# A planner that knows PSUM banks, whole-bank rows, one Strassen product later, and new places for parts of y

## The chip, the cores and the metric

The kernel runs on one core of a Trainium2 chip. The metric is the device time of one execution in microseconds. The median of three runs of the kernel before is 859.1 us (858.09 to 859.74).

## What is computed

The reference is block-causal attention followed by two feed-forward parts, in float32, on 2304 tokens of 512 features:

```python
# q, k, v: 4 batches, 8 heads, 576 positions, 64 features; blocks of 64 positions
attn = softmax(where(pos_i // 64 >= pos_j // 64, q @ k.T / 8, -1e9)) @ v
x = attn reshaped to (2304, 512)
h = (x @ w1) * (x @ w2) @ w3          # 512 -> 1024 -> 1024
x = h @ w_out                         # -> 512, called y in the kernel
h = x @ w_in                          # -> 2048
out = (relu(h) ** 2) @ w_out2         # -> 512
```

w3 and w_out are multiplied with each other first, so that the middle part is one product of the gate with that 1024 by 512 matrix.

## The kernel before, in words

**Precision.** A float32 operand is split into a high part (a copy on ScalarE) and a low part (a subtraction on VectorE), and a product is three matmuls: high by high, high by low, low by high. Every tensor that a matmul reads has therefore been through ScalarE and VectorE.

**Stages.** First the weights come in and are converted, and the eight rows of w3 times w_out (`setup_rows`, L1173) are computed, in between the attention of the first batch. Each row is a product of 128 by 512 elements that is accumulated in PSUM and then evicted: a copy on ScalarE (L1209) and a subtraction on VectorE (L1214). Rows 0 to 5 use one PSUM bank, `po`, one after the other; rows 1 to 5 are computed as two halves of 256 columns of that bank, rows 0, 6 and 7 whole. The first three rows have plain float32 operands, the others split ones. Then the first feed-forward part runs for each batch (`ab_products`, `y_products`) beside the attention of the next; y goes to DRAM.

The second feed-forward part (`second_block`, L1369 on) takes y in five blocks: block 0 of 256 tokens, blocks 1 to 4 of 512. For each pair of hidden rows j (0 to 7) a block makes a group of products. Block 0 makes them directly, blocks 1 to 4 by Strassen's scheme with seven products (`h_winograd`, L1842): P1, P7, P2, P6, P4, P5, P3 in the order of the code, each of six matmuls of 256 columns. They go into four PSUM banks in halves: `b17` has P1 on the left and P7 on the right, `b26` has P2 and P6, `b45` has P4 and P5, `b3` has P3. In blocks 2 to 4 the banks come from a ring of three (`bank3`), so P3 of a group takes the bank of P1 and P7, and P1 of the next group that of P2 and P6. ScalarE copies P1 out to `x1` (L1904), VectorE makes two sums `c1` of x1 with P6 and with P2, then `u3` out of P7 and c1, and so on (all at L1898). Blocks 2 to 4 also use Strassen's scheme for the second product (`out_strassen`, the o products, L2034).

The seven operands that a block needs of y (`b11`, `b21`, `t1`, `t2`, `t4`, `b22`, `t3`, each as high and low part) are made by `y_load` (L1522): four subtractions (L1543) and seven splits (`y_split`, L1413, by the helper at L275 and L277). Each has one buffer for all blocks, so block c+1 writes b11 only when block c has read it for the last time. The raw y of a block lies in two of four buffers (`raw`), which the output of a block uses too.

**What sets the order.** All work is written as operations with an engine, a cost, a key and lists of what they read and write (`Order.op`, L97 on). `Order.emit` (L117) plans them once, in Python, before the program exists: it goes through time with those costs and, whenever an engine is free, gives it the ready operation with the smallest key. The order in which it does so is the order of the instructions on each engine. An operation is ready when those that it depends on are done; dependencies are kept per key, and a key can be a part of a tile, such as one half of a bank. Evictions have the key `K_EVICT`, ahead of everything; in blocks 2 to 4 the adds have `K_EVICT - 1`. The work of step n of the second part has keys from K_B + 2n.

```python
start = max(t0, min(o.ready for o in todo))
o = min((o for o in todo if o.ready <= start), key=lambda o: (o.key, o.n))
```

The semaphores of the program are set afterwards from the order of the instructions, by PSUM bank and not by half.

Of the kernel before, what the change touches and what calls it, by code (L numbers as in the profile page):

```python
# [44 lines left out]
    return 128 * t + 64  # L45


class Buf:


# [16 lines left out]
class Op:  # L67
    def __init__(self, eng, cost, fn, key, spare):
        self.eng, self.cost, self.fn, self.key, self.spare = eng, cost, fn, key, spare
        self.deps = set()  # L70
        self.left = 0
        self.users = []
        self.ready = 0.0
        self.end = None


class Order:
# [19 lines left out]
    def op(self, eng, cost, fn, r=(), w=(), key=0.0, spare=0.0):  # L97

        o = Op(eng, cost, fn, key, spare)
        o.same = self.same.get(eng, 0.0)  # L100
        for k in r:
            if k in self.writer:
                o.deps.add(self.writer[k])
            self.readers.setdefault(k, []).append(o)
        for k in w:
            if k in self.writer:
                o.deps.add(self.writer[k])
            o.deps.update(self.readers.pop(k, ()))
            self.writer[k] = o
        for k in list(r) + list(w):  # L110
            if isinstance(k[0], Buf):
                k[0].ops.append(o)
        o.deps.discard(o)
        self.ops.append(o)
        return o

    def emit(self):  # L117
# [7 lines left out]
        for o in self.ops:  # L125
            o.left = len(o.deps)
            for d in o.deps:
                d.users.append(o)
        free, avail, dma = {}, {}, 0.0
        for n, o in enumerate(self.ops):  # L130
            o.n = n
            if not o.left:
                avail.setdefault(o.eng, []).append(o)
        count = 0
        while True:
            best = None
            for eng, todo in avail.items():
                if not todo:
                    continue
                t0 = free.get(eng, 0.0)  # L140
                start = max(t0, min(o.ready for o in todo))
                o = min((o for o in todo if o.ready <= start), key=lambda o: (o.key, o.n))
                if best is None or start < best[0]:
                    best = (start, o, eng)
            if best is None:
                break
            start, o, eng = best
            if eng == "P" and self.idle:
                self.idle(start - free.get(eng, 0.0))
            avail[eng].remove(o)  # L150
            count += 1
            if isinstance(o.cost, tuple):
                issue, move, late = o.cost
                free[eng] = start + issue
                dma = max(dma, start + issue) + move
                o.end = dma + late
            else:
                free[eng] = start + o.cost
                o.end = free[eng] + self.TAIL.get(eng, 0.0)
            o.fn()  # L160
            for u in o.users:
                u.left -= 1
                same = u.eng == eng and eng in "PAV"
                u.ready = max(u.ready, free[eng] + u.same if same else o.end + self.WAIT + u.spare)
                if not u.left:
                    avail.setdefault(u.eng, []).append(u)
# [4 lines left out]
def fused_kernel(ctx: ExitStack, tc: tile.TileContext, qT, kT, vp, va, w12, w3t, wo, wb, out):  # L171
# [1001 lines left out]
    def setup_rows(i):  # L1173
# [3 lines left out]
            w3o_t.append(w8_buf(8 + i // 2, f"w3o_{i // 2}"))  # L1177
        if not i:
            po_bank.append(buf("pm", "po", 1, [P, 512], F32, "po"))
        for half in range(2) if 0 < i < PO_SPLIT else (None,):  # L1180
            cols = slice(0, 512) if half is None else slice(256 * half, 256 * half + 256)
            n = cols.stop - cols.start
            if i < PO_SPLIT:
# [185 lines left out]
    def second_block():  # L1369
# [31 lines left out]
            return late("hx", [P, 512], name, F32, 1, "mb")  # L1401

        ys_ = {}
        raws_ = {}
        r_ = {}
        cp_ = {}

        def y_part(c, name):

            home = "wp" if name in ("b11", "b21") else "w2"  # L1410
            return [late(f"{name}{n}", [P, 2, TH], f"{name}{n}_{c}", F16, 1, home) for n in "hl"]

        def y_split(c, name, src, key):  # L1413
            h, l = ys_[c, name] = y_part(c, name)
            split_half(h, l, src, 2 * TH, ([(h,)], [(l,)], [key]), K_EVICT)

        def y_raw(c, key):

# [103 lines left out]
        def y_load(c):  # L1522
# [17 lines left out]
            def sub(o, x, y, r, w):  # L1540
                od.op(
                    DVE, c_dve(2 * TH),
                    lambda: dve.tensor_tensor(out=o(), in0=x(), in1=y(), op=ALU.subtract), r, w, K_EVICT,  # L1543
                )

            sub(t1, b12, b11, [k12, k11], [(t1,)])
# [19 lines left out]
        def both(f, half):  # L1566
            return [wkey(f, x, half) for x in "hl"]
# [192 lines left out]
        def h_direct(c, j, key):  # L1760
            gt = g_half(c, j, f"g2_{c}_{j}")
            bt = beta_a if j < SOON else beta
            for k in range(2):
# [8 lines left out]
                            start=n == 0, stop=n == len(mms) - 1,  # L1772
                        )

                ks = both(f, 0) + [(t,) for x in ("b11", "b21") for t in ys_[c, x]]
                od.op(PE, len(mms) * c_mm16(TH), go, ks, [(acc,)], key)
                x = buf("mo1", "a", 2, [P, GMAX], F32, f"r_{f}")
                od.op(
# [63 lines left out]
        def h_winograd(c, j, key):  # L1842
# [16 lines left out]
            def product(acc, half, left, yname, spare=0.3):  # L1859
# [8 lines left out]
                            start=n == 0, stop=n == len(mms) - 1,  # L1868
                        )

                od.op(PE, len(mms) * c_mm16(TH), go, ks + [(t,) for t in y], [(acc, half)], key, spare * strassen)

            if strassen:
                c3 = late("c", [P, 3, TH], f"c3_{c}_{j}", F32, 2)
# [24 lines left out]
                )  # L1899

            product(b17, 0, w_of(0, 0), "b11")
            product(b17, 1, s_of(3), "t3")
            od.op(
                ACT, c_act(TH), lambda: act.activation(x1(), half_of(b17, 0)(), AF.Copy), [(b17, 0)], [(x1,)], K_OUT  # L1904
            )
            product(b26, 0, w_of(0, 1), "b21")
            product(b26, 1, s_of(2), "t2")
            if strassen:
                add(TH, half_of(c1, 1), half_of(b26, 1), x1, [(b26, 1), (x1,)], ck[1:])
            else:  # L1910
# [431 lines left out]
```

## Time and profile before

| | us |
|---|---|
| median of three runs | 859.1 |
| lowest and highest | 858.09, 859.74 |
| the profiled execution | 859.63 |
| its span in the profile | 857.9 |
| TensorE matmuls busy | 834.0 (97%) |
| VectorE busy | 704.3 (82%) |
| ScalarE busy | 605.3 (71%) |

The span runs from the first instruction to the end of the last; the execution's own time has 1.7 us around it. In the rows below PE is TensorE's matmuls, PEld its weight loads, DVE is VectorE, ACT ScalarE, POOL GpSimd, which here mostly issues transfers. A row of the timeline has the start and the length in us, the engine, the line of the kernel, the operation, what it writes and reads by name, shape and count, and in brackets how long its engine had been idle and what ended that. Matmul rows last longer than their spacing, since matmuls overlap.

### The profile page before, as it was taken

What the parts mean: (1) busy time and instruction counts of PE and PEld (TensorE: products, weight loads), DVE (VectorE), ACT (ScalarE), POOL (GpSimd) and SP (SyncE); (2) the same over time, 40 slices, a digit from 0 to 9 for tenths busy, and PEclk for the clock granted to TensorE, in tenths of its full rate; (3) what the DMA queues carried; (4) which work ended last, traced back from release to release, by engine and by line L of the source; (5) the groups of instructions that cost most, each with busy time, mean ns of one, the idle gap of its engine ahead of it and who ended that gap; (6) DMA issues with size and microseconds to landing.
All of it is one profiled execution on the core that took longest, in us unless ns stands there. A gap on an engine that the chain in (4) does not pass through costs nothing. (4 is left out here: it accounts for less than half of the span.)

```text
span 857.9 us, 19317 instructions
## 1 busy us (share of the span) xinstructions
PE 834.0 (97%) x7504; PEld 676.9 (79%) x7504; DVE 704.3 (82%) x1643; ACT 605.3 (71%) x1393; POOL 111.4 (13%) x206
## 2 busy tenths in 40 slices
PE   8999999999999999999999999999999999999997
PEld 6567776778878888789979878666678888888886
DVE  5988989997787787864788899999979798797775
ACT  5988888976677676764999985756755654664562
POOL 5111211111211112001322101010020001001000
PEclk9999999999999999999999999999999999999999
DMA  8942465699998999772665512020030002001001
GB/s 312 339 150 93 135 176 161 143 182 191 215 178 159 196 154 202 134 148 77 210 193 191 176 50 74 26 100 2 1 109 16 1 2 74 2 1 51 1 2 50
DMA packets 104830, 100.23 MB, mean 117 GB/s; under 512 B 83041, under 2 KB 86881, under 8 KB 103329
## 3 DMA queue, kind: packets, MB, share of 16 engines
q0 software_dynamic: 18144, 71.18, 26.5%
q1 hardware_dynamic: 86592, 27.80, 19.1%
q8 instruction: 59, 0.97, 0.5%
q14 instruction: 35, 0.28, 0.1%
HBM read 62.78 MB, written 9.44 MB: 84 GB/s over the span
## 5 line engine op out<-in xcount | busy, mean ns | idle before, releaser
L1108 PEld LDWEIGHTS <-w 128*128 128x128 f16 x1536 | 146.8, 98 | 43.7 <-issue 5.9
L884 ACT ACTIVATE pf<-s,nm 128x192 f32<-128x192 f32 (+4 forms) x160 | 82.4, 524 | 44.0 <-DVE nm L867 39.5
L1108 PE MATMUL ab<-x0h,w 128*128 128x320 f16 x512 | 108.9, 299 | 0.5 <-DVE w L287 0.3
L1108 PE MATMUL y<-g,w3o 128*128 128x320 f32 (+1 forms) x768 | 108.3, 298 | 0.0
L1108 PEld LDWEIGHTS y<-g,w3o 128*128 128x128 f32 x768 | 103.1, 188 | 2.1 <-issue 1.2
L1108 PE MATMUL ab<-x1h,w 128*128 128x256 f16 x512 | 88.7, 273 | 0.0
L2034 PEld LDWEIGHTS <-gs 128*128 128x128 f16 x816 | 78.9, 98 | 11.4 <-DVE gs L277 2.2
L1866 PEld LDWEIGHTS <-wb 128*128 128x128 f16 x768 | 75.1, 98 | 15.2 <-issue 3.8
L1108 PE MATMUL ab<-x0l,w 128*128 128x320 f16 x256 | 76.5, 299 | 0.7 <-DVE x0l L1033 0.7
L1929 ACT ACTIVATE c<-c,beta 128x512 f32<-128x512 f32 x48 | 34.2, 713 | 58.4 <-DVE c L1898 58.4
L932 DVE SCALAR_TENSOR_TENSOR p<-pf,r,p 128x192 f16<-128x192 f32 (+2 forms) x120 | 63.0, 546 | 12.5 <-ACT p L925 11.2
L1108 PE MATMUL ab<-x1l,w 128*128 128x256 f16 x256 | 69.8, 272 | 0.0
L2161 PE MATMUL o<-wb,g 128*128 128x512 f16 x288 | 66.7, 379 | 0.6 <-DVE c L2171 0.6
L925 ACT ACTIVATE p<-pf,r 128x192 f16<-128x192 f32 (+2 forms) x120 | 62.0, 556 | 6.6 <-DMA pt<-p 3.7
L2034 PE MATMUL p<-ts,gs 128*128 128x256 f16 x480 | 61.8, 273 | 0.1
L1866 PEld LDWEIGHTS <-st 128*128 128x128 f16 x576 | 56.1, 98 | 6.7
L825 PE MATMUL s<-kraw,qraw 64*128 64x288 f32 (+4 forms) x384 | 56.5, 411 | 0.4 <-ACT pf L884 0.2
L2161 PEld LDWEIGHTS <-g 128*128 128x128 f16 x288 | 27.9, 98 | 30.3 <-issue 0.9
L825 PEld LDWEIGHTS s<-kraw,qraw 64*128 64x128 f32 x384 | 34.2, 186 | 17.1 <-issue 8.3
L2034 PE MATMUL p<-wb,gs 128*128 128x256 f16 x336 | 44.7, 273 | 0.2 <-DVE gs L277 0.2
L859 DVE TENSOR_REDUCE nm<-s 128x2 f32<-128x384 f32 (+1 forms) x64 | 42.3, 683 | 1.0
L338 DVE CUSTOM_DVE_ANT_0 cx<-raw,cx 128x1024 uint16<-128x1024 uint16 (+1 forms) x53 | 39.0, 737 | 4.5 <-ACT raw L329 2.3
(265 smaller groups left out, 1977.4 us busy)
## 6 DMA issues: line engine op xcount, KB each, us to landing
raw<-in_wb POOLq DMA_DIRECT2D x32, 512.0 KB, 5.5
raw<-in_w3t POOLq DMA_DIRECT2D x8, 1024.0 KB, 10.0
raw<-in_w POOLq DMA_DIRECT2D x16, 512.0 KB, 4.8
yraw<-ydram POOLq DMA_DIRECT2D x12, 512.0 KB, 4.5
vraw<-in_vp POOLq DMA_DIRECT2D x16, 320.0 KB, 5.3
qraw<-in_qT POOLq DMA_DIRECT2D x16, 288.0 KB, 4.7
kraw<-in_kT POOLq DMA_DIRECT2D x32, 144.0 KB, 5.9
vmix<-v SPq DMA_DIRECT2D x24, 160.0 KB, 5.0
```

Of the source, the lines that this page charges most:

```text
L338: dve.tensor_tensor(out=x(), in0=x(), in1=words()[1], op=ALU.add)
L825: pe.matmul(o[:, h] if t == 4 else o, q()[rows, q_start(t) : q_start(t) + 128], keys_()[rows, c], start=True, stop=True,)
L859: lambda k=k, t=t, nm=nm, banks=banks: dve.tensor_reduce(out=nm()[:, k], in_=banks[0]()[:, :, S_COL[t] : S_COL[t] + n_keys(t)], op=ALU.max ...
L884: act.activation(o, view(a, t), AF.Exp, bias=nm()[:, k, a : a + 1], scale=SCALE, accum_out=ssum()[:, k, a : a + 1],)
L925: lambda o=o, nk=nk, a=a, k=k, w=weights, p16=p16, r=r: act.activation(p16()[:, o : o + nk], w(a, k), AF.Copy, scale=r()[:, k, a : a + 1]),
L932: lambda o=o, nk=nk, a=a, k=k, w=weights, p16=p16, r=r: dve.scalar_tensor_tensor(out=p16()[:, o + nk : o + 2 * nk], in0=w(a, k), scalar=r( ...
L1108: pe.matmul(acc(), l, r, start=k == 0, stop=k == len(mms) - 1)
L1866: pe.matmul(acc()[:, TH * half : TH * half + TH], lhs(a, kc), y[yn]()[:, kc], start=n == 0, stop=n == len(mms) - 1,)
L1929: lambda src=src, k=k: act.activation(src(), src(), AF.Relu, scale=beta()[:, j, k : k + 1]),
L2034: pe.matmul(acc()[:, TH * u : TH * u + TH], t()[:, o : o + P], r(b), start=first and n == 0 and u == tiles[0], stop=last and n == 2 and u ...
L2161: pe.matmul(o(), g[gx]()[:, cols], wt(f)[:, a, 512:1024], start=(begin and n == 0), stop=(last and n == 2),)
```

## The change

It has four parts. The planner remembers, for each PSUM bank, until when TensorE writes it and until when the other engines use it: an operation of TensorE starts after the others are through with all of its bank, and one of another engine after TensorE's writes to any part of that bank. Rows 1 to 5 of w3 times w_out are computed in whole banks. P7 stands behind P6 in the code of a group. For block 3, b11, b21 and t3 get places of their own, in buffers that nothing else uses by then; and the subtractions and splits of y for blocks 3 and 4 have a key behind step 5 of the block before instead of `K_EVICT`.

```diff
--- before.py
+++ after.py
@@ -45,6 +45,9 @@
     return 128 * t + 64
 
 
+PSUM_POOLS = ("ps", "pm", "mb")
+
+
 class Buf:
 
 
@@ -68,6 +71,7 @@
     def __init__(self, eng, cost, fn, key, spare):
         self.eng, self.cost, self.fn, self.key, self.spare = eng, cost, fn, key, spare
         self.deps = set()
+        self.banks = ()
         self.left = 0
         self.users = []
         self.ready = 0.0
@@ -111,6 +115,7 @@
             if isinstance(k[0], Buf):
                 k[0].ops.append(o)
         o.deps.discard(o)
+        o.banks = tuple(dict.fromkeys(k[0] for k in (*r, *w) if isinstance(k[0], Buf) and k[0].pool in PSUM_POOLS))
         self.ops.append(o)
         return o
 
@@ -127,6 +132,14 @@
             for d in o.deps:
                 d.users.append(o)
         free, avail, dma = {}, {}, 0.0
+        written, read = {}, {}
+
+        def at(o):
+            t = o.ready
+            for b in o.banks:
+                t = max(t, (read if o.eng == "P" else written).get(b, 0.0))
+            return t
+
         for n, o in enumerate(self.ops):
             o.n = n
             if not o.left:
@@ -138,8 +151,8 @@
                 if not todo:
                     continue
                 t0 = free.get(eng, 0.0)
-                start = max(t0, min(o.ready for o in todo))
-                o = min((o for o in todo if o.ready <= start), key=lambda o: (o.key, o.n))
+                start = max(t0, min(at(o) for o in todo))
+                o = min((o for o in todo if at(o) <= start), key=lambda o: (o.key, o.n))
                 if best is None or start < best[0]:
                     best = (start, o, eng)
             if best is None:
@@ -157,6 +170,9 @@
             else:
                 free[eng] = start + o.cost
                 o.end = free[eng] + self.TAIL.get(eng, 0.0)
+            for b in o.banks:
+                d = written if eng == "P" else read
+                d[b] = max(d.get(b, 0.0), o.end + self.WAIT)
             o.fn()
             for u in o.users:
                 u.left -= 1
@@ -1177,7 +1193,7 @@
             w3o_t.append(w8_buf(8 + i // 2, f"w3o_{i // 2}"))
         if not i:
             po_bank.append(buf("pm", "po", 1, [P, 512], F32, "po"))
-        for half in range(2) if 0 < i < PO_SPLIT else (None,):
+        for half in (None,):
             cols = slice(0, 512) if half is None else slice(256 * half, 256 * half + 256)
             n = cols.stop - cols.start
             if i < PO_SPLIT:
@@ -1401,18 +1417,39 @@
             return late("hx", [P, 512], name, F32, 1, "mb")
 
         ys_ = {}
+        K_LOAD = [K_EVICT if c < 3 else K_B + 2 * (KP * (c - 1) + 5) + 0.55 for c in range(len(BLOCKS))]
         raws_ = {}
         r_ = {}
         cp_ = {}
 
+        OTHER_HOMES = {
+            "b11": ("wp", "ysq", 1, 1), "b21": ("wp", "ysc", 1, 1), "t3": ("mo1", "a", 2, 2),
+        }
+
+        class Piece:
+            def __init__(self, b, n):
+                self.b, self.n, self.key = b, n, (b, n)
+
+            def __call__(self):
+                return self.b()[:, self.n]
+
+        def key_of(t):
+            return t.key if isinstance(t, Piece) else (t,)
+
         def y_part(c, name):
 
+            if c == FIRST_S + 1 and name in OTHER_HOMES:
+                *home, pieces = OTHER_HOMES[name]
+                if pieces == 2:
+                    return [buf(*home, [P, 2, TH], F16, f"{name}{n}_{c}") for n in "hl"]
+                t = buf(*home, [P, 2, 2, TH], F16, f"{name}_{c}")
+                return [Piece(t, n) for n in range(2)]
             home = "wp" if name in ("b11", "b21") else "w2"
             return [late(f"{name}{n}", [P, 2, TH], f"{name}{n}_{c}", F16, 1, home) for n in "hl"]
 
         def y_split(c, name, src, key):
             h, l = ys_[c, name] = y_part(c, name)
-            split_half(h, l, src, 2 * TH, ([(h,)], [(l,)], [key]), K_EVICT)
+            split_half(h, l, src, 2 * TH, ([key_of(h)], [key_of(l)], [key]), K_LOAD[c])
 
         def y_raw(c, key):
 
@@ -1540,7 +1577,7 @@
             def sub(o, x, y, r, w):
                 od.op(
                     DVE, c_dve(2 * TH),
-                    lambda: dve.tensor_tensor(out=o(), in0=x(), in1=y(), op=ALU.subtract), r, w, K_EVICT,
+                    lambda: dve.tensor_tensor(out=o(), in0=x(), in1=y(), op=ALU.subtract), r, w, K_LOAD[c],
                 )
 
             sub(t1, b12, b11, [k12, k11], [(t1,)])
@@ -1772,7 +1809,7 @@
                             start=n == 0, stop=n == len(mms) - 1,
                         )
 
-                ks = both(f, 0) + [(t,) for x in ("b11", "b21") for t in ys_[c, x]]
+                ks = both(f, 0) + [key_of(t) for x in ("b11", "b21") for t in ys_[c, x]]
                 od.op(PE, len(mms) * c_mm16(TH), go, ks, [(acc,)], key)
                 x = buf("mo1", "a", 2, [P, GMAX], F32, f"r_{f}")
                 od.op(
@@ -1868,7 +1905,7 @@
                             start=n == 0, stop=n == len(mms) - 1,
                         )
 
-                od.op(PE, len(mms) * c_mm16(TH), go, ks + [(t,) for t in y], [(acc, half)], key, spare * strassen)
+                od.op(PE, len(mms) * c_mm16(TH), go, ks + [key_of(t) for t in y], [(acc, half)], key, spare * strassen)
 
             if strassen:
                 c3 = late("c", [P, 3, TH], f"c3_{c}_{j}", F32, 2)
@@ -1899,12 +1936,12 @@
                 )
 
             product(b17, 0, w_of(0, 0), "b11")
-            product(b17, 1, s_of(3), "t3")
             od.op(
                 ACT, c_act(TH), lambda: act.activation(x1(), half_of(b17, 0)(), AF.Copy), [(b17, 0)], [(x1,)], K_OUT
             )
             product(b26, 0, w_of(0, 1), "b21")
             product(b26, 1, s_of(2), "t2")
+            product(b17, 1, s_of(3), "t3")
             if strassen:
                 add(TH, half_of(c1, 1), half_of(b26, 1), x1, [(b26, 1), (x1,)], ck[1:])
             else:
```

## Rows read from the trace of the kernel before

**Rows 1.** The page's part 1, busy time of each engine.

```profile
PE 834.0 (97%) x7504; PEld 676.9 (79%) x7504; DVE 704.3 (82%) x1643; ACT 605.3 (71%) x1393; POOL 111.4 (13%) x206
```

**Rows 2.** The table of windows: busy us of each engine, TensorE's granted clock, DMA.

```profile
36.00:64.00 28.00, 24.70 (x128) 17.70 (x129) 22.88 (x43) 23.89 (x45) 3.67 (x6) 0.94 0.49 167
64.00:124.00 60.00, 58.15 (x473) 46.45 (x470) 51.47 (x131) 50.03 (x135) 10.50 (x20) 1.00 0.42 126
124.00:200.00 76.00, 71.12 (x684) 55.72 (x683) 70.29 (x191) 62.76 (x158) 11.99 (x23) 1.00 0.76 165
200.00:600.00 400.00, 397.95 (x3763) 320.81 (x3760) 325.63 (x790) 296.00 (x731) 60.96 (x111) 1.00 0.62 141
600.00:840.00 240.00, 237.09 (x2078) 202.17 (x2077) 197.44 (x405) 143.43 (x263) 9.46 (x16) 1.00 0.07 23
690.00:700.00 10.00, 8.75 (x81) 7.68 (x80) 9.96 (x21) 3.80 (x8) 0.00 (x0) 1.00 0.01 2
700.00:765.00 65.00, 65.00 (x594) 57.47 (x593) 52.84 (x111) 39.50 (x73) 2.91 (x5) 1.00 0.08 26
```

**Rows 3.** Waits of TensorE: us in total, times, longest us.

```profile
PE p L1866 <- DVE c L1898: 2.9, 3, 1.3
...
PE po L1108 <- DVE w3o L1214: 2.4, 5, 0.6
...
PE pv_bank L357 <- DVE wsum L406: 1.7, 2, 1.3
```

**Rows 4.** Timeline of an ordinary group of block 2: start us, us, instruction [idle before].

```profile
665.90 0.27 PE L1866 MATMUL p<-b11h,wb 128*128 128x256 f16 x1
...
666.55 0.27 PE L1866 MATMUL p<-t3h,st 128*128 128x256 f16 x1
...
666.86 0.39 ACT L1904 ACTIVATE x<-p 128x256 f32<-128x256 f32 x1 [0.53 <-PE p L1866]
```

**Rows 5.** Timeline of the turn from block 2 to block 3.

```profile
690.63 0.68 DVE L1543 TENSOR_TENSOR yraw<-yraw,t 128x512 f32<-128x512 f32 x1
...
690.67 0.36 ACT L1904 ACTIVATE x<-p 128x256 f32<-128x256 f32 x1
...
691.57 0.41 DVE L1898 TENSOR_TENSOR c<-p,x 128x256 f32<-128x256 f32 x1
...
691.90 0.68 DVE L1940 TENSOR_TENSOR s<-c 128x512 f32<-128x512 f32 x1
...
692.50 0.41 DVE L1898 TENSOR_TENSOR c<-p,x 128x256 f32<-128x256 f32 x1
...
692.96 0.27 PE L1866 MATMUL p<-b11h,wb 128*128 128x256 f16 x1 [1.25 <-DVE c L1898]
...
695.91 0.68 DVE L277 TENSOR_TENSOR t3l<-yraw,t3h 128x512 f16<-128x512 f32 x1
```

**Rows 6.** Timeline of the rows' stage, VectorE, ScalarE and TensorE.

```profile
36.84 0.61 ACT L1209 ACTIVATE w3o<-po 128x512 fp32r<-128x512 f32 x1
...
37.93 0.69 DVE L1214 TENSOR_TENSOR w3o<-po,w3o 128x512 fp32r<-128x512 f32 x1
...
45.20 0.38 ACT L1209 ACTIVATE w3o<-po 128x256 fp32r<-128x256 f32 x1 [0.81 <-PE po L1108]
...
45.63 1.13 PE L1108 MATMUL po<-wox,w3x 128*128 128x256 f32 x4 [0.47 <-ACT w3o L1209]
...
46.87 0.42 DVE L1214 TENSOR_TENSOR w3o<-po,w3o 128x256 fp32r<-128x256 f32 x1 [1.59 <-PE po L1108]
```

**Rows 7.** Timeline of TensorE, two runs of row matmuls.

```profile
73.58 2.35 PE L1108 MATMUL po<-wo,w 128*128 128x256 f32 x18
...
113.97 7.28 PE L1108 MATMUL po<-wo,w 128*128 128x512 f32 x30
```

**Rows 8.** The page's part 5, ScalarE's longest kind in the Strassen blocks.

```profile
L1929 ACT ACTIVATE c<-c,beta 128x512 f32<-128x512 f32 x48 | 34.2, 713 | 58.4 <-DVE c L1898 58.4
```


## The prediction

> **What bounds the kernel now.** I read the page's busy time first: TensorE's matmuls cover 834.0 of 857.9 us of span [rows 1]. So all that can be won without less matmul work is the 23.9 us in which TensorE is idle, and the question is where these lie and which of them the change touches. The table of windows answers the first half [rows 2]: 36 to 64 us has 3.3 us idle (28.0 less 24.7), 64 to 124 has 1.85, 124 to 200 has 4.9, the 400 us after that 2.05, and 600 to 840 has 2.9; what is left (about 9 us) is the start before 36 us and the tail after 840 us, which the change hardly reaches. VectorE is second: nearly full at 124 to 200 (70.3 of 76 us), 82% busy from 600 to 840.
>
> The table of waits names the idle stretches [rows 3]: the Strassen products wait for VectorE's adds at L1898, 2.9 us in 3 times; the rows of w3 times w_out wait for VectorE's eviction at L1214, 2.4 us in 5; the small norm matmul waits for wsum, 1.7 us in 2. The first is all of the idle time of 600 to 840.
>
> Two stretches of the timeline show why. In an ordinary group [rows 4] P1 (b11) writes the left half of bank p17 and its last matmul starts at 665.90; ScalarE's copy of that half starts only at 666.86, when P7 (t3), which writes the right half, has had its last matmul (666.55 plus 0.27). So two halves of one bank are not used by two engines at once, though the planner in the code (`Order.emit`) knows only the halves' own dependencies. At the turn from block 2 to 3 [rows 5] the copy is at 690.67, VectorE then does a subtraction of the load of y (690.63), one add out of p26 (691.57), a 0.68 us step of another group (691.90), and only then the second add (692.50); the next P1, which takes p26's bank, starts at 692.96 after 1.25 us idle. VectorE has 9.96 of 10 us busy there, against 52.8 of 65 in the 65 us behind it [rows 2].
>
> **The change part by part.**
>
> *Order, with P7 behind P6.* No instruction is added. Products have the same six matmuls; P7 starts two products later, and one product is 6 matmuls of 0.11 us, 0.65 us (P1's and P7's last starts are 0.65 apart [rows 4]). The copy x1 can then run during P2 and P6, and both adds out of p26 can start 0.65 us earlier counted from the group's own start, while P7 runs; u3 waits for P7's end, which is where P6 ended before. The pair of adds no longer comes apart in VectorE's order, since the planner now knows that both can start only after P6. In ordinary groups TensorE does not wait, so I cost this at nothing there: the cover is the matmuls of the o products, which fill the span (2.9 us idle in 240). P7, though, now needs x1 to have finished reading; that is the new wait, and behind it in TensorE's order stand P4, P5 and the o products. From P1's end it has two products, 1.3 us, for a copy of 0.39 us [rows 4]. With one instruction ahead of it on ScalarE, the longest is 0.71 us [rows 8], it takes 1.1 us and TensorE does not wait.
>
> *The y of blocks 3 and 4.* For each, 4 subtractions and 7 splits on VectorE and 7 copies on ScalarE move from the highest priority to one below every eviction; no DMA moves. The splits of b11, b21 and t3 of block 3 no longer wait until block 2 has finished with the same buffers (and those of block 4 find the old places empty). In the trace t3's last part is done only at 695.91 [rows 5], seven us after block 3's first product, so P7 was skipped at the turn; now it can fill 0.65 us there. At the turn VectorE keeps 5 load steps of 8. The time that the rest takes is there: 12.2 us of 65 idle [rows 2]. Price if it is not taken up: the raw y buffers, which these steps free, are those of block 2's output and of POOL's next loads, so late steps hold the output's adds; I take that as hidden because b11 and t3, the first buffer's last readers, come earlier.
>
> Together these two parts take away the 2.9 us of waits on L1898 [rows 3]; the bounds are 2.9 us and nothing. With P7 ready and the adds ahead of the load, the chain that held P1 loses the 0.68 us step and a load step, more than the 1.25 us idle together with P7's 0.65 us. I take **2.7 us**.
>
> *Whole rows.* Rows 1 to 5 had two halves of 256 columns in one bank. The trace shows that they alternate with the evictions [rows 6]: ScalarE's copy of a half had waited 0.81 us for TensorE, TensorE's next half waits 0.47 us for that copy, VectorE waits 1.59 us for TensorE. Per row the bank was out of use for two pairs of 0.38 and 0.42 us, now for one of 0.61 and 0.69 us: 1.6 against 1.3 us, and one turn of waits instead of two. Five rows save 1.5 us on VectorE and ScalarE together. For TensorE's own time, 18 matmuls of 256 columns ran in 2.35 us, 30 of 512 in 7.28 us [rows 7]: per row of 24 wide ones 5.8 us either way, so weights loaded half as often bring nothing. What remains is idle time. Bounds: all of the 5.15 us of 36 to 124 [rows 2] gone, or the new pair of 1.3 us open in each of five rows, 6.5 us, less the 2.4 us waited now [rows 3]: 4.1 us lost. The value lies near the 2.4 us that is waited for these evictions, since the planner now gives TensorE scores, transposes and weighted sums during an eviction: I take **1.8 us** off. It reaches the end only if TensorE has a backlog behind the rows: it has, 7.28 us of rows 6 and 7 without a pause, right before the first products with w1 and w2 [rows 7].
>
> *Order elsewhere.* The only other bank in parts is the one of the weighted sums, which also takes the norm columns. Nothing shows a wait there for the bank itself; its 1.7 us is for data that came late [rows 3]. Bounds 1.7 us off and as much on; I take nothing.
>
> **Sum.** 2.7 + 1.8 = 4.5 us. The profiled execution took 859.6 us around its span of 857.9; 859.6 - 4.5 = 855.1. It stands 0.5 us over the median of 859.1, so **854.6 us** for the median.
>
> **The rivals.** (a) *The rows' gain is eaten.* From 124 us on the first block needs w1 and w2 converted, by a VectorE 92% busy [rows 2]; TensorE arriving earlier would wait there. For it: 4.9 us idle in that window already. Against it: of these only 1.7 us are waits for wsum in VectorE's hands. 859.1 - 2.7 = 856.4 us.
> (b) *All goes.* 2.9, 3.5 of the 5.15, and the norm's 1.7: 8.1 us, 851.0 us.
> (c) *P7 waits for the copy.* Where ScalarE has two instructions in front of x1, at 0.71 us the most each, the copy ends 1.8 us after P1 and TensorE stands 0.5 us, which it never did before. There are 32 groups (8 in each of 4 blocks). In half of them that is 8 us: 859.1 - 4.5 + 8 = 862.6 us, slower; it decides from 4.5 us, 9 groups of the 32. For it: at the turn the copy came late, at 690.67, behind the load's own. Against it: ScalarE is 60% busy from 600 to 840 [rows 2], and the planner gives the copy the highest priority.
> (d) *The clock.* The window 36 to 64 has a granted clock of 0.94 [rows 2], that is 3.4 us at 1.2 instead of 2.4 GHz, 1.7 us lost, behind a pause of TensorE. If one longer eviction per row brought two more such dips and the rows gained nothing: 859.1 - 2.7 + 3.4 = 859.8 us. The Trainium skill (TensorE: Matmul & The Clock Gate, section "A second HAM failure mode: psum-queue depth-cycling") says that a kernel which cycles through its banks with small pauses between groups of matmuls can have its clock go up and down. By that rule one bank for five rows is a poor place for longer pauses; the trace agrees as far as its one dip in the rows' stage goes, while the Strassen stage, with three banks in turn, shows none (1.00 [rows 2]).
> (e) *The order hardly differs*, because the planner's durations are off by more than the halves' waits: 859 us.
>
> **How the numbers follow.** The forecast has 0.44, (a) 0.22, (b) 0.10, (c) 0.10, (d) 0.08, (e) 0.06. A measurement of this kernel tells 0.2% from no change, 1.7 us: faster is below 857.4, slower above 860.8. Faster: the forecast, nearly all of (a), and (b), 0.74; the same: (d), most of (e), the edge of (a), 0.15; slower: (c) and a little of (d), 0.11. The range must leave out (c) and may leave out part of (d): 850.8, just under (b), to 859.3.
>
> **What would show it.** Right: no wait of the products on L1898 at the turns and VectorE below 9.9 of 10 us there; 600 to 840 with under 1 us of TensorE idle; the copy x1 starting within 0.7 us of P1's end with P7 behind P6; the evictions of rows (by the code 13, 10 of them 256 wide) become 8, all 512 wide, TensorE's wait on L1214 below 1 us and 36 to 124 with about 3.3 us idle; the start of the products with w1 and w2 about 2 us earlier. Wrong: TensorE waiting on L1904 (then (c)); more idle time at 124 to 200 (then (a)); a clock under 0.94 in the rows' stage (then (d)); new waits of products for the splits of t1, t2, t4 or b22.

## The result, and the profile after the change

The changed kernel takes **850.93 us** (median of 4 runs, 850.54 to 851.87) against 858.96 us (858.09 to 859.74) for the kernel before: a ratio of 0.9908, 95% interval 0.9891 to 0.9926. That is 8.0 us off, where 4.5 were forecast. The profiled execution took 851.08 us around a span of 849.3. Line numbers below are those of the changed kernel: its rows' matmuls stand at L1124 (before L1108), their evictions at L1225 and L1230 (L1209 and L1214), the products at L1903 (L1866), the adds out of product banks at L1935 (L1898), the copy x1 at L1940 (L1904), the small norm matmul at L373 (L357) and VectorE's read of it at L379 (L363).

The page's busy time after the change, which answers to [rows 1]:

```profile
PE 830.0 (98%) x7400; PEld 666.7 (78%) x7400; DVE 702.2 (83%) x1638; ACT 605.1 (71%) x1388; POOL 110.8 (13%) x206
```

TensorE is busy for 4.0 us less and idle for 4.6 us less (849.3 less 830.0 is 19.3, before 23.9). The table of windows, the same stretches as in [rows 2] (busy us of TensorE, its weight loads, VectorE, ScalarE and POOL, then the granted clock, the DMA share and GB/s):

```profile
36.00:64.00 28.00, 26.34 (x121) 13.86 (x120) 26.35 (x47) 27.79 (x54) 3.64 (x6) 1.00 0.49 167
64.00:124.00 60.00, 56.14 (x388) 40.61 (x385) 49.66 (x129) 49.01 (x130) 10.73 (x20) 0.97 0.45 137
124.00:200.00 76.00, 72.67 (x701) 58.17 (x702) 70.46 (x194) 60.29 (x151) 11.91 (x22) 1.00 0.80 171
200.00:600.00 400.00, 398.66 (x3767) 320.12 (x3766) 327.87 (x791) 298.86 (x739) 60.65 (x110) 1.00 0.59 138
600.00:840.00 240.00, 239.38 (x2117) 206.51 (x2115) 198.06 (x407) 142.54 (x259) 9.46 (x16) 1.00 0.07 23
```

TensorE's idle time, window by window, before and after: 3.3 and 1.7 us; 1.85 and 3.9; 4.9 and 3.3; 2.05 and 1.3; 2.9 and 0.6. So the Strassen blocks (600 to 840) have lost nearly all of theirs, but the rows' stage has not: 64 to 124 has more than before. Between 36 and 600 us the idle time is 12.1 us before and 10.2 after, only 1.9 less. The table of waits, TensorE's rows that answer to [rows 3]:

```profile
PE po L1124 <- DVE w3o L1230: 3.2, 3, 2.2
...
PE pv_bank L373 <- ACT junk L429: 1.9, 2, 1.2
PE pv_bank L373 <- DVE x0l L1049: 1.4, 1, 1.4
...
PE p L1903 <- ACT x L1940: 0.5, 2, 0.2
```

No product waits for L1935 any more. The rows still wait for VectorE's eviction, 3.2 us in 3 times instead of 2.4 in 5. The longest of these waits in the timeline (start us, us, instruction, idle before):

```profile
88.38 0.57 ACT L1225 ACTIVATE w3o<-po 128x512 fp32r<-128x512 f32 x1
...
89.55 0.68 DVE L1230 TENSOR_TENSOR w3o<-po,w3o 128x512 fp32r<-128x512 f32 x1
...
90.29 2.31 PE L1124 MATMUL po<-wo,w 128*128 128x512 f32 x6 [2.18 <-DVE w3o L1230]
```

Row 5 needs the one bank that row 4 leaves, and that bank is read by two engines in turn; VectorE's step came 0.6 us after ScalarE's copy had ended. Where the time came from is seen best by cutting the execution at the first product of block 1, the first block in Strassen's scheme. TensorE's timeline, the kernel before:

```profile
544.08 0.27 PE L1866 MATMUL p<-b11h,wb 128*128 128x256 f16 x1
```

and the changed kernel:

```profile
538.44 0.27 PE L1903 MATMUL p<-b11h,wb 128*128 128x256 f16 x1
```

Up to there 5.6 us are gone, of which about 1.9 are the idle time above. The rest is time in which TensorE counts as busy; the products of the rows have 2.8 us of it (58.5 us of TensorE before, 55.7 after, summed over the groups that write `po`). From there to the end of the span it is 313.8 us before (857.9 less 544.08) and 310.9 after, 2.9 us less. I call these two stretches the **early** and the **late** one.

The early order has changed, too. The first product with w1 and w2, before:

```profile
123.87 0.31 PE L1108 MATMUL ab<-x0h,w 128*128 128x320 f16 x1
```

and after:

```profile
105.40 0.31 PE L1124 MATMUL ab<-x0h,w 128*128 128x320 f16 x1
```

Before, these products came behind the last row; now they begin 18.5 us earlier, and rows 6 and 7 come behind the first of them.

The turn from block 2 to 3, to be read against [rows 5], in the changed kernel's timeline:

```profile
683.16 1.47 PE L1903 MATMUL p<-b,wb 128*128 128x256 f16 x12
...
684.94 0.36 ACT L1940 ACTIVATE x<-p 128x256 f32<-128x256 f32 x1
685.01 0.27 PE L1903 MATMUL p<-t2h,st 128*128 128x256 f16 x1
...
685.36 0.27 PE L1903 MATMUL p<-t3h,st 128*128 128x256 f16 x1
...
686.80 0.75 DVE L1935 TENSOR_TENSOR c<-p,x 128x256 f32<-128x256 f32 x2
...
687.32 0.82 PE L2071 MATMUL p<-wb,gs 128*128 128x256 f16 x6
```

P1 and P2 run as one train of 12 matmuls, the copy x1 runs during P6 (t2) and is done before P7 (t3) begins, the two adds are one pair, and TensorE goes on without a pause. An ordinary group, to be read against [rows 4]:

```profile
667.87 0.27 PE L1903 MATMUL p<-b11h,wb 128*128 128x256 f16 x1
...
668.43 0.36 ACT L1940 ACTIVATE x<-p 128x256 f32<-128x256 f32 x1
...
669.29 0.27 PE L1903 MATMUL p<-t3h,st 128*128 128x256 f16 x1
```

The copy starts 0.3 us after P1's last matmul has ended (667.87 plus 0.27) and is done 0.5 us before P7's first.

### The profile page after: what moved, and what is told of

It reads as the page before. It is cut to its first block, busy times and chain, and to the rows that moved or that the text cites. A ratio compares the mean times of both kernels' runs of the same rounds, so it can differ in the third digit from the quotient of the medians.

```text
span 849.3 us, 19120 instructions
## 1 busy us (share of the span) xinstructions
PE 830.0 (98%) x7400; PEld 666.7 (78%) x7400; DVE 702.2 (83%) x1638; ACT 605.1 (71%) x1388; POOL 110.8 (13%) x206
## 5 line engine op out<-in xcount | busy, mean ns | idle before, releaser
L1124 PEld LDWEIGHTS <-w 128*128 128x128 f16 x1536 | 146.7, 98 | 42.8 <-issue 5.4
L1124 PE MATMUL ab<-x0h,w 128*128 128x320 f16 x512 | 109.9, 299 | 0.1
L1124 PE MATMUL y<-g,w3o 128*128 128x320 f32 (+1 forms) x768 | 108.1, 298 | 0.0
L1124 PEld LDWEIGHTS y<-g,w3o 128*128 128x128 f32 x768 | 103.2, 188 | 2.2 <-issue 1.5
L1124 PE MATMUL ab<-x1h,w 128*128 128x256 f16 x512 | 88.7, 273 | 0.0
L1903 PEld LDWEIGHTS <-wb 128*128 128x128 f16 x768 | 75.2, 98 | 11.3 <-issue 0.5
L1124 PE MATMUL ab<-x0l,w 128*128 128x320 f16 x256 | 76.5, 299 | 0.0
L1124 PE MATMUL ab<-x1l,w 128*128 128x256 f16 x256 | 69.8, 272 | 0.0
L1903 PEld LDWEIGHTS <-st 128*128 128x128 f16 x576 | 56.1, 98 | 8.4 <-issue 1.6
L841 PE MATMUL s<-kraw,qraw 64*128 64x288 f32 (+4 forms) x384 | 54.5, 409 | 0.2 <-ACT pf L900 0.2
L291 ACT ACTIVATE gs<-c 128x512 f16<-128x512 f32 (+1 forms) x56 | 29.9, 535 | 18.6 <-DVE c L1977 18.4
```

The lines of the kernel that those rows point to most:

```text
L291: od.op(ACT, c_act(n), lambda: act.activation(hi(), src(), AF.Copy), ks, kh, key)
L841: pe.matmul(o[:, h] if t == 4 else o, q()[rows, q_start(t) : q_start(t) + 128], keys_()[rows, c], start=True, stop=True,)
L1124: pe.matmul(acc(), l, r, start=k == 0, stop=k == len(mms) - 1)
L1903: pe.matmul(acc()[:, TH * half : TH * half + TH], lhs(a, kc), y[yn]()[:, kc], start=n == 0, stop=n == len(mms) - 1,)
```

## The experiments

The change has four parts, so they were tried first one by one on the kernel before, then taken one by one out of the changed kernel. A kernel with all four switched off is the kernel before; every kernel below is written as a difference to it ("before and ...") or to the changed kernel ("after, but ..."). All were timed in five rounds. The kernel before had a median of 858.95 us beside the first four, 858.84 beside the second four and 859.34 beside the third four. "Early" is the start of block 1's first product, "late" the span less that, both of the one profiled execution.

### Each part alone on top of the kernel before

**Whole rows alone.**

```diff
-        for half in range(2) if 0 < i < PO_SPLIT else (None,):
+        for half in (None,):
```

> Theory A (the early gain of 5.6 us is the rows' own: one turn of evictions per row, and wider matmuls): 4 us or more below before, about 855, and the part from block 1 of the second feed-forward on (its first Strassen product at 544.1 us in before) as long as before. Rival B (whole rows pay only if the planner knows the banks): under 1.5 us, about 858, with new waits for L1214 in the rows' stage.

Measured: 864.27 us, ratio 1.0057 (1.0039 to 1.0076): **5.3 us slower**. Early 549.96, late 314.1. Neither theory had that. The edit that was to bring 1.8 us costs three times as much where it stands alone. Its windows in the early stretch:

```profile
64.00:124.00 60.00, 55.09 (x375) 40.33 (x375) 50.51 (x128) 48.13 (x129) 10.97 (x20) 0.94 0.42 134
124.00:200.00 76.00, 70.95 (x679) 54.68 (x677) 67.24 (x187) 60.59 (x152) 11.52 (x21) 1.00 0.76 168
```

Idle time is 4.9 and 5.05 us there (before 1.85 and 4.9), and the granted clock of the first stretch is 0.94.

**The planner's knowledge of banks alone.**

```diff
-                start = max(t0, min(o.ready for o in todo))
-                o = min((o for o in todo if o.ready <= start), key=lambda o: (o.key, o.n))
+                start = max(t0, min(at(o) for o in todo))
+                o = min((o for o in todo if at(o) <= start), key=lambda o: (o.key, o.n))
```

> Theory A: the planner's knowledge alone sets the pair of adds right in the Strassen blocks, so that most of the 2.9 us idle there goes, and little before: 1.5 to 3 us below before, 856 to 857.5. Rival B: with rows still in halves it now plans TensorE's other work into the evictions, so the early part gains 2 us or more too: about 854.5.

Measured: 858.58 us, ratio 0.9997 (0.998 to 1.0013): no difference. Early 542.87, late 315.0. The wait that it was to help with is still there; its row among TensorE's waits:

```profile
PE p L1903 <- DVE c L1935: 2.6, 3, 1.2
```

So at the turns it is not the planner's ignorance of halves that holds P1.

**P7 behind P6 alone.**

```diff
             product(b17, 0, w_of(0, 0), "b11")
-            product(b17, 1, s_of(3), "t3")
...
             product(b26, 1, s_of(2), "t2")
+            product(b17, 1, s_of(3), "t3")
```

> Theory A: P7 behind P6 alone brings the copy x1 and the adds forward by 0.65 us in each group, but the load of y keeps its priority at the turns: about 1 us off, 858. Rival B: the planner, without banks, lets P7 run into the copy: TensorE waits for L1904 in several groups, and the time is the same or longer, 859 to 861.

Measured: 857.64 us, ratio 0.9989 (0.9974 to 1.0004): 1.3 us less at the median, within the interval of no change. Late 313.2, 0.6 us less than before. The two waits that matter:

```profile
PE p L1903 <- DVE c L1935: 1.0, 2, 0.5
PE p L1903 <- ACT x L1940: 0.6, 2, 0.4
```

The wait for the adds falls from 2.9 us to 1.0, and the new wait for the copy x1 is 0.6 us in 2 of 32 groups: rival (c) needed 9 groups.

**The y of blocks 3 and 4 alone** (late priority for its load, and places of its own for three parts of block 3).

```diff
+        K_LOAD = [K_EVICT if c < 3 else K_B + 2 * (KP * (c - 1) + 5) + 0.55 for c in range(len(BLOCKS))]
...
+            if c == FIRST_S + 1 and name in OTHER_HOMES:
```

> Theory A: the load of y out of the adds' way removes the two turns' waits of 1.25 and 1.29 us and not much else: about 2 us off, 857. Rival B: without the pair of adds in the right order the second add still stands behind a 0.68 us step: half of it, 858.

Measured: 855.97 us, ratio 0.9958 (0.9932 to 0.9984): **3.0 us faster**. Late 311.4, 2.4 less than before. The window of the Strassen blocks:

```profile
600.00:840.00 240.00, 239.39 (x2094) 203.57 (x2092) 200.08 (x410) 143.39 (x261) 9.47 (x16) 1.00 0.07 23
```

0.6 us idle, as in the changed kernel. (Its profiled execution took 860.30 us, 4.3 over its median, and has its early stretch at 547.15; its early order is that of the kernel before, so I read only the late stretch of it.)

### Each part taken out of the changed kernel

**After, but rows in halves** (`for half in range(2) if 0 < i < PO_SPLIT else (None,)` again).

> After, with the rows in halves again. Theory A (rows and planner pay only together in the early part, as rows alone were 5 us slower and the planner alone nothing): the early 5.6 us are gone, the 3.0 us of the Strassen blocks stay: about 856. Rival B (the planner with P7 and y does more than alone): 853 to 854.

Measured: 855.43 us, ratio 0.9956 (0.9944 to 0.9968). Early 541.49, late 310.8. Without the whole rows 4.5 of the 8.0 us are missing, all of it early.

**After, but the planner blind to banks** (`o.ready` again in place of `at(o)`, both lines).

> After, with the planner that knows no banks. Theory A: whole rows without the planner's knowledge cost 5 us as in the run with rows alone, while P7 and y keep their 2 to 3 us: about 861. Rival B (the cost of whole rows was an accident of that order): 855 or less.

Measured: 861.48 us, ratio 1.0037 (1.0022 to 1.0051): slower than the kernel before, and 10.5 us slower than the changed one. Early 547.49, late 311.0: late it loses nothing. The part that does nothing alone is worth most beside whole rows. Its windows:

```profile
64.00:124.00 60.00, 53.00 (x379) 38.89 (x379) 51.25 (x131) 48.85 (x130) 11.51 (x21) 1.00 0.43 137
124.00:200.00 76.00, 70.96 (x681) 54.82 (x680) 67.24 (x188) 59.85 (x151) 11.00 (x20) 1.00 0.76 167
200.00:600.00 400.00, 395.75 (x3737) 319.30 (x3736) 325.08 (x783) 297.03 (x733) 61.33 (x111) 1.00 0.59 139
```

Idle time: 7.0, 5.0 and 4.25 us, against 3.9, 3.3 and 1.3 in the changed kernel, 7.8 us more, at the full clock. Its timeline shows one place where it arises:

```profile
111.81 0.97 PE L1087 MATMUL pv_bank<-pt,vraw 128*64 128x128 f32 x12
...
112.86 0.47 ACT L300 ACTIVATE x1h<-pv_bank,sx 128x256 f16<-128x256 f32 x1
...
115.30 0.48 DVE L303 SCALAR_TENSOR_TENSOR x1l<-pv_bank,sx,x1h 128x256 f16<-128x256 f32 x1
...
115.83 0.16 PE L373 MATMUL pv_bank<-wsum,ones 128*128 128x2 bf16 x1 [1.46 <-DVE x1l L303]
```

The bank of the weighted sums also holds two columns for the norms. The norm matmul reads only wsum and writes only its columns, so it has no dependency on x1l; yet it starts only when x1l's eviction (115.30 plus 0.48) has left the bank. Not all of its 1.46 us is the bank's, though. VectorE finished wsum itself only at 115.39:

```profile
115.16 0.23 DVE L422 TENSOR_TENSOR wsum<-wsum 128x1 f32<-128x1 f32 x2
```

So at most 0.4 us of that wait is for the bank, the rest for data that came late. And the reverse, in the group of VectorE's reads of these columns (the row under it says until when the engine sat idle before it):

```profile
L379 DVE TENSOR_SCALAR nh<-pv_bank x9: 148/152/159, 20.4 to 172.3; 128x2 int32<-128x2 int32 x8, 128x1 int32<-128x1 int32 x1
...
  PE pv_bank L1033: 2.3, 1
```

VectorE, the second busiest engine, stood 2.3 us before a 0.15 us read until the weighted sums (L1033) had left the bank. Behind that read ScalarE waits for VectorE and then TensorE for ScalarE:

```profile
172.68 1.33 ACT L300 ACTIVATE w<-cx,wsc 128x512 f16<-128x512 f32 x2 [1.75 <-DVE wsc L281]
...
174.78 1.73 PE L841 MATMUL s<-kraw,qraw 64*128 64x192 f32 x10 [0.83 <-ACT pf L900]
```

In the changed kernel no idle time stands before L379. A wait of the first kind is still there, behind an eviction of x0l:

```profile
169.50 0.19 ACT L429 ACTIVATION_READ_ACCUMULATOR junk<-cx 128x1 f32 x1
169.51 0.54 DVE L1049 SCALAR_TENSOR_TENSOR x0l<-pv_bank,vback,x0h 128x320 f16<-128x320 f32 x1
...
170.11 0.18 PE L373 MATMUL pv_bank<-wsum,ones 128*128 128x2 bf16 x1 [1.41 <-DVE x0l L1049]
```

There, too, the sums were ready (169.69) 0.4 us before the bank. So waits of the first kind stand in both kernels; only VectorE's is gone.

**After, but P7 before P2** (its line moved back).

> After, with P7 in front of P6 again. Theory A: the planner and y already remove the waits at the turns, P7 adds the 0.65 us of slack that nobody needs: within 1 us of after, 851 to 852. Rival B: without P7 in its new place the adds are late again at the turns: 853 or more, with waits for VectorE's adds.

Measured: 852.58 us, ratio 0.9917 (0.9901 to 0.9933). Early 539.23, late 311.4, 0.5 more than the changed kernel's. At the median that is 1.65 us, but the intervals of the two ratios overlap.

**After, but y loaded as before** (`K_LOAD` all `K_EVICT`, `OTHER_HOMES` unused).

> After, with y of blocks 3 and 4 at its old priority and places. Theory A (y alone gave the turns' 2.5 us): about 853.5, with TensorE idle 2 us or more at the two turns. Rival B (the planner and P7 suffice): 851.5.

Measured: 853.79 us, ratio 0.9941 (0.9919 to 0.9964), early 538.34, late 313.6: 2.7 us back, and the wait with it:

```profile
PE p L1903 <- DVE c L1935: 2.1, 2, 1.3
```

### Which banks, which half of the edit, and a smaller ring

**After, but the planner knows only the banks of the attention's pool "ps"** (the scores' and that of the weighted sums).

```diff
-PSUM_POOLS = ("ps", "pm", "mb")
+PSUM_POOLS = ("ps",)
```

> After, but the planner keeps only the banks of the attention's pool (in it one bank has parts: that of the weighted sums, with the norm columns). Theory A (the 10 us between after and the same without the planner's knowledge lie in that one bank): within 1 us of after, 850 to 852. Rival B (they lie in the halves of the Strassen banks, or need both): 855 or more.

Measured: 851.7 us, ratio 0.9917 (0.9888 to 0.9945). Early 538.46, late 310.7: the changed kernel within 0.2 us in both. At the median it is 0.8 us more, but the intervals of the two ratios overlap: no worth of knowing the rows' bank and the product banks shows.

**After, but the planner knows all banks other than these** (`PSUM_POOLS = ("pm", "mb")`).

> After, but the planner keeps only the other banks (those of the rows and of the Strassen products). Theory A: as slow as after without the planner's knowledge, 860 to 862, with VectorE waiting for the weighted sums when it reads a norm column. Rival B: 851 to 854.

Measured: 861.49 us, ratio 1.0012 (0.9991 to 1.0032). Early 547.11, late 310.7: as with a blind planner. The order of TensorE's work up to block 1 is the same, instruction by instruction, in this kernel and in the one with the blind planner; and in the one with "ps" alone it is that of the changed kernel.

**After, but block 3's parts in their old places** (late priority kept).

```diff
-            if c == FIRST_S + 1 and name in OTHER_HOMES:
+            if c < 0:
```

> After, with the late key of the load of y but the old places. Theory A (it was the priority): as after, 851. Rival B (it was the places, which let three splits of eight go before the turn): TensorE waits at the turns as without both, about 853.5. If both are needed the late key alone may be worse than neither: over 854.

Measured: 854.25 us, ratio 0.9937 (0.9915 to 0.996). Late 313.7, as with y loaded as before, and the Strassen window has its idle time back:

```profile
600.00:840.00 240.00, 236.91 (x2090) 203.84 (x2088) 196.38 (x402) 141.52 (x257) 9.47 (x16) 1.00 0.07 23
```

So the late priority without the places brings nothing. The places without it were not tried.

**After, but row 5 not in the rows' one bank** (it goes to the ring of banks that the later rows use), to see what the 2.18 us wait of row 5 costs.

```diff
-    PO_SPLIT = 6
+    PO_SPLIT = 5
```

> After, with row 5 of w3 times w_out behind the first batch's attention and in the ring of three banks, as rows 6 and 7, so that it no longer waits 2.2 us for row 4's eviction. Theory A (that wait, and the half clock behind it, reach the end): 848 to 849.5. Rival B (TensorE meets the next wait, for w1 and w2, instead): as after, or slower where the order behind it shifts: 851 to 854.

Measured: 861.87 us, ratio 1.0014 (0.9988 to 1.0039). Early 549.88, late 310.7. Row 5's wait is gone, but at the same place (90.73 us) TensorE now stands 2.2 us before transposes. The window 64 to 124 of this kernel:

```profile
64.00:124.00 60.00, 54.79 (x355) 38.68 (x355) 47.25 (x122) 45.74 (x124) 11.25 (x21) 0.89 0.41 123
```

The first of TensorE's waits in it:

```profile
PE tp L984 <- ACT pt L990: 4.2, 4, 2.2
PE pv_bank L373 <- ACT junk L429: 3.1, 3, 1.5
PE ab L1124 <- ACT ys L1329: 2.1, 1, 2.1
```

And behind that a long stretch of half clock:

```profile
92.00:107.00 15.00, 13.61 (x61) 8.31 (x61) 11.86 (x29) 9.13 (x26) 4.30 (x8) 0.54 0.60 186
```

A wait of 2.2 us in the profile was no 2.2 us to be had: with it gone, rows, transposes and weighted sums come in another order, and the kernel is 11 us slower. How much of that is the order itself and how much the clock is open. By the clock of the two windows 64 to 124, 0.89 and 0.97, TensorE loses 6.6 us of full speed here and 1.8 in the changed kernel, 4.8 more (an estimate from these two rows). This dip belongs to the kernel: all 12 executions have a mean granted clock of 0.990 to 0.992, the changed kernel's four 0.996 to 0.998.

### What the runs add up to

| kernel | rows | planner | P7 | y | median us | early us | late us |
|---|---|---|---|---|---|---|---|
| before | halves | blind | old | old | 858.96 | 544.1 | 313.8 |
| before and planner | halves | banks | old | old | 858.58 | 542.9 | 315.0 |
| before and rows | whole | blind | old | old | 864.27 | 550.0 | 314.1 |
| before and P7 | halves | blind | new | old | 857.64 | 542.2 | 313.2 |
| before and y | halves | blind | old | new | 855.97 | (547.2) | 311.4 |
| after, halves | halves | banks | new | new | 855.43 | 541.5 | 310.8 |
| after, blind | whole | blind | new | new | 861.48 | 547.5 | 311.0 |
| after, P7 old | whole | banks | old | new | 852.58 | 539.2 | 311.4 |
| after, y old | whole | banks | new | old | 853.79 | 538.3 | 313.6 |
| after | whole | banks | new | new | 850.93 | 538.4 | 310.9 |

The late stretch is a matter of y: 313.2 to 315.0 us in the five kernels with the old load, 310.8 to 311.4 in the five with the new one; P7's place is worth about 0.5 us in it. The early stretch is a matter of rows and planner together: halves 541.5 to 544.1 with either planner (but for the bracketed one), whole rows 547.5 to 550.0 with the blind one and 538.3 to 539.2 with the one that knows banks. One profile's early stretch is a rough number: the three kernels whose early order is that of the kernel before have 544.1, 542.2 and 547.2. By the medians whole rows are worth +5.3 us with the blind planner and -4.5 with the other.

## Why the prediction was right, and where it was not

The direction and the range held: 850.9 lies at the fast edge of 850.8 to 859.3, at the number of rival (b), 851.0, which had a chance of 0.10. It is not (b)'s sum, though, whose norm wait and eviction waits were to vanish: of these terms only the one on L1898 did. The number came from a gain of the early stretch that no part of the prediction has, so that it lies in the range at all (0.1 us inside its edge) is luck.

**The Strassen term, 2.7 us, was right in size and wrong in one part of its cause.** It measured 2.9 us (late, 313.8 to 310.9). The steps "the adds ahead of the load" and "with P7 ready" hold: y alone takes 2.4 us off and P7's place 0.6. The step "the pair of adds no longer comes apart in VectorE's order, since the planner now knows" fails: with the planner's knowledge alone the wait on L1935 is 2.6 us, and without it (after, but blind) the late stretch is as good as in the changed kernel. One of the marks set for it was no mark: VectorE below 9.9 of 10 us at the turn. The 10 us from the first product of block 3 in the changed kernel:

```profile
683.00:693.00 10.00, 9.93 (x92) 8.75 (x91) 9.87 (x21) 7.96 (x15) 0.00 (x0) 1.00 0.00 1
```

VectorE is below 9.9 by 0.03 us alone, as full as before (9.96 [rows 2]), and TensorE is full too: what mattered was which of VectorE's steps came first. The price of the raw buffers held later did not appear (0.6 us idle in the whole window of the Strassen blocks), as was assumed. The cost of P7's new wait, set at nothing in ordinary groups, was 0.5 us in 2 of 32 groups: rival (c) is out.

**The term of the whole rows, 1.8 us, was mis-sized, and for a reason that was not in it.** It measured 4.5 us by the medians (855.43 to 850.93), 3.1 by the early stretch of the two profiles. But none of it came as said. "What remains is idle time" fails: of these 3.1 us only about 0.7 are idle time between 36 and 600 us (10.9 us with halves, 10.2 after); where the others lie is open. "5.8 us either way" is a slip: 18 matmuls in 2.35 us make 6.3 us for a row of 48 narrow ones. At full clock the products of all rows take 55.5 us of TensorE with halves (after, halves) and 54.4 whole (after, blind), 1.1 us that the sum put at nothing. The wait on the rows' eviction did not fall below 1 us; it rose to 3.2. The evictions are 8, all 512 wide, and start at 37.8 to 123.9 us:

```profile
L1230 DVE TENSOR_TENSOR w3o<-po,w3o x8: 679/682/690, 37.8 to 123.9; 128x512 fp32r<-128x512 f32 x8
```

36 to 124 has 5.5 us idle (1.7 and 3.9), not 3.3. The products with w1 and w2 begin 18.5 us earlier, not 2, and no longer behind "a backlog" of rows 6 and 7. The clause "since the planner now gives TensorE scores, transposes and weighted sums during an eviction" also fails in its reason: without knowing the rows' bank at all (knowing only pool "ps") the time is the same but for 0.8 us, which is within the noise.

**The step that failed is "Order elsewhere": "Nothing shows a wait there for the bank itself ... I take nothing".** It was true of the kernel before, and it is true of halves: there the planner's knowledge is worth 0.4 us at the median. It is not true once the rows are whole. Then the order of the early stretch is another, and whether the planner knows the banks of pool "ps" decides over 10.5 us. The prediction added four edits up; for two of them the worth of one depends on the other (whole rows +5.3 us under the blind planner, -4.5 under the other). The bound set for this step, 1.7 us either way, came from a wait of the old order and could not hold for a new one.

How far the cause is shown: that the gain hangs on the planner knowing the banks of pool "ps" is shown by the pair of runs that splits the pools. The scores' banks are in the same pool and no run separates them, but the code does: every operation on the scores has the key of its whole tile (L824 on), so the planner knew those dependencies already, and the bank of the weighted sums is the only one in "ps" of which it learns something new. How the 10.5 us come about is shown in small part only. In the blind order that bank costs TensorE at most 0.4 us in the one wait above and 0.8 us in the chain behind the other. The rest of the 7.8 us of more idle time is waits at many lines, none longer than 2.0 us; I have not traced them back to these two. And whole rows were seen in three early orders only (538 us, 547 to 550 us, and 550 us with row 5 in the ring), so a part of the difference may be an accident of order that another small edit would undo.

**The other rivals.** (a) is out: 124 to 200 lost idle time (4.9 to 3.3 us). (d): the clock is 1.00 instead of 0.94 in 36 to 64, and 0.97 instead of 1.00 in 64 to 124, behind the 2.18 us wait above: one dip before, one after, no more. In the kernel with row 5 in the ring it was 0.89, with 5.2 us idle in that window; but the kernel with the blind planner had 7.0 us idle there at 1.00, so more pauses alone did not bring more dips. The Trainium skill (TensorE: Matmul & The Clock Gate, "A second HAM failure mode: psum-queue depth-cycling"), by which small pauses between groups of matmuls can make the clock go up and down, is neither borne out nor refuted by that; the rows' one bank by itself brought no more dips. (e) names the time of the planner on the kernel before, 858.6 us, but not its reason: the early order does differ there (TensorE has 3.4 us idle in 64 to 124 and 3.8 in 124 to 200, before 1.85 and 4.9), and it all but cancels.

The Trainium skill (PSUM — Partial Sum Buffer, "PSUM bank collisions raise a hardware error") says to guard PSUM with semaphores by bank and quadrant (32 partitions), or more simply by bank, and not by address. The trace agrees with a kernel that does so: the norm matmul starts 0.05 us after an eviction of other columns has ended (115.78 and 115.83), though its own sums were there at 115.39. What the runs add is what it costs when whoever plans the order does not plan by the same rule: 10.5 us with whole rows, nothing that shows with halves.

## What to carry to other kernels

A planner that orders engines should know every resource that the program's semaphores guard, and the cheapest tenant can count: here two norm columns in a bank of weighted sums. Edits that change an order are to be priced together with the order, not added up: of these four, one was worth +5.3 us alone and -4.5 in company. A lower priority for a load may bring nothing if the buffers it fills are still those that the running block reads; here the two brought 2.7 us together and the priority alone none.

## What the runs showed that was not expected

A stretch of half clock comes and goes between executions that have the same instructions in the same order there. The window 36 to 64 of the kernel before and P7 alone, whose order there is the kernel before's (its row in [rows 2] has a clock of 0.94):

```profile
36.00:64.00 28.00, 24.69 (x140) 17.97 (x140) 24.52 (x46) 25.48 (x48) 3.71 (x7) 1.00 0.48 165
```

and of the changed kernel with P7 before P2, whose order there is the changed kernel's (1.00 above):

```profile
36.00:64.00 28.00, 26.33 (x108) 12.90 (x107) 25.25 (x45) 26.59 (x48) 4.11 (x7) 0.94 0.56 185
```

So one profile's clock row doesn't tell whether a dip belongs to the kernel; it took the rows of several kernels with the same order to see that this one belongs to neither. The dip of the kernel with row 5 in the ring, in all its 12 executions, is of the other kind.
